# Sliding-window attention and a highway layer in one kernel: key halves by head, one pass of value products, and a new order of the work

## The chip, the core and the metric

The kernel runs on one core of a Trainium2 chip. The metric is the time of one execution on the device in microseconds (us); lower is better. The time shown is the median of several executions. A separate execution is taken with the profiler on, and all rows below come from it. The engines are TensorE (PE in the rows, with its weight loads as PEld), VectorE (DVE), ScalarE (ACT), GpSimd (POOL) and SyncE (SP). Each works through its own queue in order, and semaphores hold an instruction back until what it needs is there.

## What is computed

Eight batches of eight heads, 576 positions, 64 values a head; attention looks back over a window of 128 positions, with a slope for each head on the distance. Its output, as 4,608 tokens of 512 values, goes through a highway layer.

```python
scores = scale * np.matmul(q, k.transpose(0, 1, 3, 2))
rel = pos[:, None] - pos[None, :]
slopes = 2.0 ** (-8.0 * (np.arange(H, dtype=np.float32) + 1) / H)
mask = (rel >= 0) & (rel < window)
scores = np.where(mask, scores - slopes[:, None, None] * np.abs(rel), -1e9)
attn = np.exp(scores - max); attn = attn / (np.sum(attn) + 1e-09)
x = np.matmul(attn, v)             # then tokens x 512
H = np.maximum(x @ w_h, 0.0)
T = 1.0 / (1.0 + np.exp(-(x @ w_t + b_t)))
out = T * H + (1.0 - T) * x
```

## The kernel before

The work is cut in two ways. A **unit** (b, s) is a batch and one of four stretches of keys: two key tiles of 64 (three in the last stretch), against the 192 queries that can see each tile. There are 32 units. A **block** is 128 rows of output: (b, 0) to (b, 3) for each batch, and after each pair of batches a fifth, (b, 4), with the last 64 rows of both. There are 36 blocks. A block takes keys from its own unit and from the one before.

The order of all work is written out by hand: in `ORDER` every letter is one step, and the loop at L386 issues the steps of a letter one after the other. So the string sets the order on each engine's queue. The steps are:

- `L` load (L117), GpSimd's queue: q and k of a batch in two DMAs each, one for the even heads and one for the odd ones (batch 0 in halves of the positions, so eight), v in one. Weights are loaded once.
- `T` tr (L199), VectorE: transposes q (w = 0) or k (w = 1) of a batch in 32 x 32 blocks of words, 18 times.
- `s` scores (L216), TensorE: 32 to 48 matmuls of 32 rows x 64 columns. Which half of PSUM's partitions a key tile lands in depends on its head and its number: `half = (j + a) % 2` (L223).
- `e` soft (L238), ScalarE: exp of 1,536 scores a partition, and `m` mask (L245), VectorE: multiplies all 1,536 by `MK`, a table that holds the slopes' exponentials and the window.
- `p`, `D`, `P` (L249 to L285): the value products in two phases of 16 matmuls with a drain of TensorE between them. v lies in SBUF in its natural tiles of 128 rows, so a key tile's half is that of v. Two row halves of the array must not write one PSUM bank at a time; each phase pairs bank j with half `(j + odd) % 2`.
- `n` norm (L287), VectorE: reciprocal of the sums, which a column of ones in v gives (L291), and the product (L292).
- `x` x_tr (L298), TensorE: transposes x into a PSUM tile `f`; `c` x_copy (L304), ScalarE, to SBUF.
- `b` bias (L329), ScalarE, writes the bias into a tile `f`; `z` mm_z (L334) adds the gate product; `h` mm_h (L308) the H product, four matmuls each of 128 x 128 against 512 columns.
- `a` tanh (L346) and `r` relu (L321), ScalarE; `v` sub (L325), `y` to_gate_v (L353), `g` gate (L357), VectorE; `o` add_x (L360), GpSimd, in two halves from block 18 on; `d` store (L368), SyncE's queue.

PSUM holds one tile of scores (four banks), one of values `av` (two banks) and two tiles `f` (L98), which transposed x, gate product and H product take in turn. In SBUF q and k have three buffers, v four (`NVA`), exp'd scores eight (`NP`), x eight, and the tiles of the highway layer six each.

The mask table is made in setup3 and setup4 (L166 to L192): eight exps on ScalarE, a product on VectorE, and copies on GpSimd for the last unit's form.

Of the kernel before, what the change touches and what calls it, by code (L numbers as in the profile page):

```python
# [11 lines left out]
NLD, NTR, NVA, NP = 3, 3, 4, 8  # L12
# [4 lines left out]
GATE_S = ()  # L17

HALF_O = set()

ORDER = (
    "L1LLLLLLLLTLTLsLeTLLTLsL2e3seLsemLmpDP4mnmxpcLDP5LznLhayxrpLTDPcbzLhnaTxLrpcDPbnszeyvghv"
    "gamoxrscoydpbDPeznLdhvLgamxrsoTcpbDPeLdznhamxLrsLcvpTbDPeznhamxrsvcvpbyDPLgeyzonhaLmdxrs"
    "yycTpbDPezLhnaxLrmscvbpDPvegLznohgaxdrsmcpbDPgvoeznhoTdaxrpLdmDPcbsnzLeyghuoaxLdscmbpDPv"
    "eyzyLnLhamxrysyvcpgDPbgeznohgdamxrsgocTpbDPeLdzhLnarmxpcDPTobzodnhayxdrysyvcgpbDPvgeznoh"
    "TadxrscpbDPmezLnhyamxLrsycTopbDPeznLdhLvamLxrsgcvLpbgDPvegznohaTxrosdcpbDPmdeznohaTxdrsc"
    "mpbDPeyznhuaxscmbpDPezynhyamxrsyycvpbvDPgegznohaTodxrscpdbDPmeznhamxrsycyvpbgDPgezvnohag"
    "dxmrscpyobTDPezodnhamdxrscyvpbDPgvezgnohaxmdrscopbDPezndhyamxrysvcgpbvDPgeoznhaodxrsmcdp"
    "bDPyevznhvamxrsvcgpDPbggeznohaoudxpcDPmdbznohavdyxgrpyDPcobnzdvghayoxrpDPcgdbynozhvdagyx"
    "orpDPcbndzvghaoxrvdcybgzohadyrvgod"  # L30
# [3 lines left out]
def lists():  # L34

    units = [(b, s) for b in range(NB) for s in range(NS)]
    blocks = []
    for m in range(NB // 2):
        blocks += [(b, s) for b in (2 * m, 2 * m + 1) for s in range(NS)] + [(2 * m, NS)]
    trs = [(0, i, w) for i in range(2) for w in range(2)]  # L40
    trs += [(b, None, w) for b in range(1, NB) for w in range(2)]
    loads = [("t", 0, i, w, j) for i in range(2) for w in range(2) for j in range(2)]
    loads[8:8] = [("v", 0)]
    loads += [("w", 0), ("w", 1), ("w", 2)]
    for b in range(1, NB):
        loads += [("t", b, None, w, j) for w in range(2) for j in range(2)] + [("v", b)]
    by = dict(L=loads, T=trs)
    by.update({k: units for k in "sem"})
    by.update({k: blocks for k in "pPnxchzagod"})
    n = dict(enumerate(blocks))  # L50
    HALF_O.update(blocks[NB * 2 + 2 :])
    by["u"] = [n[i] for i in n if i not in RELU_S]
    by["r"] = by["v"] = [n[i] for i in n if i in RELU_S]
    by["b"] = [n[i] for i in n if i in BIAS_S]
    by["t"] = [n[i] for i in n if i in GATE_S]
    by["y"] = [n[i] for i in n if i not in GATE_S]
    return by
# [3 lines left out]
def kernel(  # L61
# [36 lines left out]
    ps_f = ctx.enter_context(tc.tile_pool(name="ps_f", bufs=2, space=PSUM))  # L98
# [9 lines left out]
    PB = [cp.tile([P, 64 + 256 * H], BF16, name=f"p{i}") for i in range(NP)]  # L108
# [6 lines left out]
    MK = [cp.tile([P, H, 192], BF16, name=f"mk{i}") for i in range(2)]  # L115

    def load(kind, *at):  # L117
        if kind == "t":
            b, i, w, j = at
            ld = LD[b % NLD, w]  # L120
            src = (q, k)[w][b].rearrange("(g j) n d -> j g n d", j=2)[j]
            if i is None:
                nc.gpsimd.dma_start(
                    out=ld[j::2].rearrange("p t d -> p (t d)"),
                    in_=src.rearrange("g (s t) d -> g s (t d)", t=NT))
            else:
                n = NT // 2
                nc.gpsimd.dma_start(  # L128
                    out=ld[j::2, i * n : (i + 1) * n, :].rearrange("p t d -> p (t d)"),
                    in_=src[:, i * 288 : (i + 1) * 288].rearrange(  # L130
                        "g (s t) d -> g s (t d)", t=n))
# [12 lines left out]

    def setup1():

        for i in range(NP):
            nc.vector.memset(PB[i][:, 0:64], 0.0)
            nc.vector.memset(PB[i][:, 64:].rearrange("p (h n) -> p h n", h=H)[:, :, 192:256], 0.0)
# [6 lines left out]
    rel_i = cp.tile([P, 192], I32, name="rel_i")  # L156
    dia_i = cp.tile([P, P], I32, name="dia_i")

    def setup2():

        for i in range(2):
            nc.gpsimd.iota(rel_i[i * D : (i + 1) * D, :], pattern=[[1, 192]], base=0,
                           channel_multiplier=-1)
        nc.gpsimd.iota(dia_i[:], pattern=[[1, P]], base=0, channel_multiplier=-1)

    def setup3():  # L166

        rel = cp.tile([P, 192], F32, name="rel")
        win = cp.tile([P, 192], BF16, name="win")
        ok = cp.tile([P, 192], BF16, name="ok")  # L170
        dia = cp.tile([P, P], F32, name="dia")
        nc.vector.tensor_copy(out=rel[:], in_=rel_i[:])
        for h in range(H):
            nc.scalar.activation(out=MK[0][:, h, :], in_=rel[:], func=ACTF.Exp,
                                 scale=-slopes[h])
# [8 lines left out]
        nc.vector.tensor_tensor(  # L184
            out=MK[0][:], in0=MK[0][:],
            in1=ok[:].rearrange("p (o n) -> p o n", o=1).to_broadcast([P, H, 192]), op=ALU.mult)

    def setup4():
        nc.gpsimd.tensor_copy(out=MK[1][:], in_=MK[0][:])
        for j in range(2):  # L190
            rows = slice((1 - j) * D, (2 - j) * D)
            nc.gpsimd.tensor_copy(out=MK[1][rows, j::2, 128:192], in_=MK[0][rows, 1 - j :: 2, 0:64])  # L192

    def setup5():
        pb = ps_f.tile([P, DM], F32, name="f")
# [3 lines left out]
    def tr(b, i, w):  # L199
        n = slice(0, NT) if i is None else slice(i * NT // 2, (i + 1) * NT // 2)  # L200
# [3 lines left out]
        if w:  # L204
            to = to[:, 2 * s0 : 2 * (s0 + 16 * t)].rearrange("p (s t j) -> p t s j", t=t, j=2)
# [8 lines left out]
    SC, PT, AV, X = {}, {}, {}, {}  # L214

    def scores(b, s):  # L216
        sc = SC[b, s] = ps_sc.tile([P, G, 512], F32, name="sc")
        QT = TR[b % NTR, 0][:].rearrange("p (j n) e -> p n j e", j=2)
        KT = TR[b % NTR, 1][:].rearrange("p (n j) e -> p n j e", j=2)
        for a in (2 * s, 2 * s + 1) if s < 3 else (6, 7, 8):  # L220
            for e in range(2):
                for j in range(2):
                    half = (j + a) % 2  # L223
                    n = min(192, S - a * D)
                    off = 192 * j if a < 8 else 192 * (1 - j) + 128
                    for g in range(G):
                        rows = slice(32 * g, 32 * g + 32)
                        nc.tensor.matmul(  # L228
                            out=sc[half * D : (half + 1) * D, g, off : off + n],
                            lhsT=KT[rows, a * D : (a + 1) * D, j, e],  # L230
                            rhs=QT[rows, a * D : a * D + n, j, e],
                            start=e == 0, stop=e == 1,
                            tile_position=(32 * g, half * D))

    def pview(t):
        return t[:, 64:].rearrange("p (h n) -> p h n", h=H)[:, :, 0:192]

    def soft(b, s):  # L238
        t = PT[b, s] = PB[(b * NS + s) % NP]
        nc.scalar.activation(  # L240
            out=pview(t).rearrange("p (g j) n -> p g j n", j=2),
            in_=SC.pop((b, s))[:, :, 0:384].rearrange("p g (j n) -> p g j n", j=2),
            func=ACTF.Exp, scale=scale)

    def mask(b, s):  # L245
        p = pview(PT[b, s])
        nc.vector.tensor_tensor(out=p, in0=p, in1=MK[s == 3][:], op=ALU.mult)  # L247

    def pv(b, s, odd=0):  # L249

        if not odd:
            AV[b, s] = ps_av.tile([P, 2, 512], F32, name="av")
        av = AV[b, s]
        for g in range(G):
            todo = []
            for j in range(2):
                half = (j + odd) % 2
                at = 64 + 256 * (2 * g + j)
                if s < NS:
                    own = (b, s, 2 * s + odd, at - 64 * odd, 0, P)  # L260
                    last = (b, s - 1, 2 * s - 2 + odd, at + 128 - 64 * odd, 0, P)
# [161 lines left out]
```

## Time and profile before

| | |
|---|---|
| median of 3 runs | 186.24 us (185.04 to 187.01) |
| the profiled execution, its own time | 184.66 us |
| its span, first to last instruction | 182.8 us |
| mean granted TensorE clock | 0.965 of full speed |
| GpSimd adds (L365) | 54 instructions, 50.8 us |
| DMA, software queue / hardware queue | 15.24 MB / 9.44 MB |

Spans and starts are in us from the first instruction of the profiled execution. A row of a group gives line, engine, operation, output and inputs with their shapes, the count, then busy us and the mean ns of one, then the idle time ahead of it and what ended it. A row of the timeline gives start, duration and the same names. A row of windows gives the stretch, then the busy us of PE, PEld, DVE, ACT and POOL with their counts, the granted clock and DMA. A row of waits gives who waited for whom: us in total, times, the longest. A busy share is an average over stages with different limits.

### The profile page before, as it was taken

The page shows a single profiled execution, that of the slowest core. Times are in us where ns is not written, and L with a number is a line of the kernel's source. Part 1 is how long each engine was busy: PE and PEld are TensorE (multiplying, and loading weights), DVE is VectorE, ACT ScalarE, POOL GpSimd, SP SyncE. Part 2 cuts the span into 40 slices and gives each one's busy share as a digit, 9 for nine tenths or more (in the row PEclk, how much of TensorE's full clock was granted, in tenths as well). Part 3 has the DMA queues.
Part 4 walks back from the last instruction along what each step waited for, and adds up shares of the span by engine and source line. Part 5 has one row for each costly group of instructions (what it writes and reads, how often), then busy time and mean ns, then how long its engine had stood idle before and what let it go on. Part 6 is the DMA issues. An engine that isn't in the chain of part 4 may idle for free.

```text
span 182.8 us, 6167 instructions
## 1 busy us (share of the span) xinstructions
PE 130.7 (71%) x2674; PEld 73.8 (40%) x2674; DVE 143.2 (78%) x260; ACT 123.1 (67%) x182; POOL 94.8 (52%) x111
## 2 busy tenths in 40 slices
PE   0002337897894999899399969989997899888530
PEld 0001224453462556555245544445554456444310
DVE  7027196589994899899989999989999799887520
ACT  2003852488894799889339975989997999756620
POOL 7684589108923198559210995005092742948350
PEclk9999999999997899999969987999999999999997
DMA  1899999999999999999961699990422213333122
GB/s 17 102 177 161 207 201 148 149 154 156 232 194 145 180 127 162 226 231 180 233 157 66 47 185 175 244 108 10 113 84 95 77 42 118 95 129 126 71 105 59
DMA packets 53147, 25.07 MB, mean 137 GB/s; under 512 B 45184, under 2 KB 46208, under 8 KB 53120
## 3 DMA queue, kind: packets, MB, share of 16 engines
q0 software_dynamic: 47872, 15.24, 96.4%
q1 hardware_dynamic: 5248, 9.44, 15.5%
q8 instruction: 21, 0.34, 0.8%
q14 instruction: 6, 0.05, 0.1%
HBM read 30.41 MB, written 9.44 MB: 218 GB/s over the span
## 4 chain that ended last, share of the span: by engine, by line
DVE 37%; PE 32%; ACT 13%; issue 7%; DMA 5%; POOL 3%; POOLq 0%; DVEq 0%
PE f L340 12%; DVE p L247 9%; PE f L312 9%; DVE tr L209 8%; DVE uu L358 6%; DVE x L292 5%; DMA ld<-in_k_dram 5%; PE av L278 4%; ACT f L332 4%; ACT rr L323 3%; DVE tt L354 3%; PE sc L228 3%; DVE uu L327 3%; ACT xt L306 3%; POOL ld L128 2%
## 5 line engine op out<-in xcount | busy, mean ns | idle before, releaser
L365 POOL TENSOR_TENSOR ot<-uu,x 128x256 f32<-128x256 bf16 (+1 forms) x54 | 50.8, 960 | 64.4 <-issue 33.2
L240 ACT ACTIVATE p<-sc 128x1536 bf16<-128x1536 f32 x32 | 46.7, 1458 | 16.7 <-PE sc L228 16.6
L340 PE MATMUL f<-wT,xt 128*128 128x512 bf16 x144 | 40.6, 407 | 6.0 <-ACT f L332 5.1
L312 PE MATMUL f<-wH,xt 128*128 128x512 bf16 x144 | 39.1, 396 | 0.0
L209 DVE STREAM_TRANSPOSE tr<-ld 128x1152 uint32<-128x1152 uint32 (+1 forms) x18 | 29.6, 1657 | 8.9 <-DMA ld<-in_q_dram 7.9
L228 PE MATMUL sc<-tr,tr 32*64 32x192 bf16 (+2 forms) x1152 | 21.0, 262 | 21.5 <-DVE tr L209 15.6
L278 PE MATMUL av<-va,p 64*128 64x65 bf16 (+1 forms) x1088 | 29.2, 196 | 7.1 <-issue 2.5
L247 DVE TENSOR_TENSOR p<-p,mk 128x1536 bf16<-128x1536 bf16 x32 | 33.8, 1060 | 0.3 <-ACT p L240 0.2
L348 ACT ACTIVATE tt<-f 128x512 f16<-128x512 f32 x36 | 21.7, 602 | 16.1 <-PE f L340 14.5
L306 ACT COPY xt<-f 128x512 bf16<-128x512 bf16 x36 | 21.0, 583 | 9.6 <-PE f L301 9.4
L292 DVE TENSOR_TENSOR x<-av,rd 128x512 bf16<-128x512 f32 x36 | 24.9, 692 | 3.0
L278 PEld LDWEIGHTS <-p 64*128 64x128 bf16 (+1 forms) x1088 | 20.3, 98 | 15.4 <-issue 10.3
L323 ACT ACTIVATE rr<-f 128x512 bf16<-128x512 f32 x33 | 19.7, 598 | 8.6 <-PE f L312 7.2
L228 PEld LDWEIGHTS <-tr 32*64 32x64 bf16 x1152 | 15.0, 138 | 25.2 <-DVE tr L209 16.1
L358 DVE TENSOR_TENSOR uu<-uu,tt 128x512 bf16<-128x512 bf16 x36 | 22.8, 644 | 0.7
L312 PEld LDWEIGHTS <-xt 128*128 128x128 bf16 x144 | 14.8, 103 | 19.4 <-issue 4.1
L134 POOL DMA_DIRECT2D va<-in_v_dram x8 | 15.0, 1870 | 14.6 <-PE av L278 10.5
L301 PE MATMUL f<-ident,x 128*128 128x128 bf16 x144 | 14.2, 222 | 10.1 <-DVE x L292 9.9
L332 ACT COPY f<-bB 128x512 f32<-128x512 f32 x35 | 21.2, 606 | 0.0
L340 PEld LDWEIGHTS <-xt 128*128 128x128 bf16 x144 | 13.0, 101 | 18.0 <-issue 6.2
L301 PEld LDWEIGHTS <-x 128*128 128x128 bf16 x144 | 10.5, 99 | 22.8 <-DVE x L292 14.6
L354 DVE TENSOR_SCALAR tt<-tt 128x512 f16<-128x512 f16 x36 | 14.9, 424 | 5.5 <-ACT tt L348 5.5
(38 smaller groups left out, 64.5 us busy)
## 6 DMA issues: line engine op xcount, KB each, us to landing
out_dram<-ot SPq DMA_DIRECT2D x32, 256.0 KB, 3.8
va<-in_v_dram POOLq DMA_DIRECT2D x8, 576.0 KB, 14.3
ld<-in_q_dram POOLq DMA_DIRECT2D x14, 288.0 KB, 13.9
ld<-in_k_dram POOLq DMA_DIRECT2D x14, 288.0 KB, 13.4
out_dram<-ot SPq DMA_DIRECT2D x8, 128.0 KB, 2.4
ld<-in_q_dram POOLq DMA_DIRECT2D x4, 144.0 KB, 7.1
ld<-in_k_dram POOLq DMA_DIRECT2D x4, 144.0 KB, 8.2
wH<-in_moe_w_h_dram POOLq DMA_DIRECT2D x1, 512.0 KB, 11.2
```

Source lines behind the costliest of these rows:

```text
L209: nc.vector.transpose(out=to, in_=LD[b % NLD, w][:, n].rearrange("p t d -> p (t d)").bitcast(U32).rearrange("p (t i) -> p t i", i=32))
L228: nc.tensor.matmul(out=sc[half * D : (half + 1) * D, g, off : off + n], lhsT=KT[rows, a * D : (a + 1) * D, j, e], rhs=QT[rows, a * D : a * ...
L240: nc.scalar.activation(out=pview(t).rearrange("p (g j) n -> p g j n", j=2), in_=SC.pop((b, s))[:, :, 0:384].rearrange("p g (j n) -> p g j ...
L247: nc.vector.tensor_tensor(out=p, in0=p, in1=MK[s == 3][:], op=ALU.mult)
L278: nc.tensor.matmul(out=av[o : o + n, j, g * (D + 1) : (g + 1) * (D + 1)], lhsT=PT[bb, ss][rows, col : col + n], rhs=VA[bb % NVA][rows, (9 ...
L292: nc.vector.tensor_tensor(out=x[:].rearrange("p (g j d) -> p j g d", j=2, d=D), in0=av[:, :, :, 0:D], in1=rd[:].to_broadcast([P, 2, G, D]) ...
L306: nc.scalar.copy(out=xt[:].rearrange("p c n -> p (c n)"), in_=XP.pop(at)[:, 0:512])
L312: nc.tensor.matmul(out=pa[:], lhsT=xt[:, c, :], rhs=wH[:, c, :], start=c == 0, stop=c == NC - 1)
L332: nc.scalar.copy(out=pz[:], in_=bB[:])
L340: nc.tensor.matmul(out=PZ[at][:], lhsT=xt[:, c, :], rhs=wT[:, c, :], start=c == 0 and not begun, stop=begun and c == NC - 1, skip_group_ch ...
L358: nc.vector.tensor_tensor(out=UU[at][:], in0=UU[at][:], in1=TT.pop(at)[:], op=ALU.mult)
L365: nc.gpsimd.tensor_tensor(out=ot[:, i : i + n], in0=uu[:, i : i + n], in1=x[:, i : i + n], op=ALU.add)
```

## The change

1. **Halves by head.** A key tile's half is now its head's parity `j`, for scores, exp'd scores and mask alike. q is loaded by one DMA a batch with a head's 16 partitions together; so is k of batch 0, while k of the other batches keeps two DMAs and the old layout. The transposition of q writes `p t j s` instead of `p t s j`.
2. **Odd v tiles copied.** For odd key tiles v lies in the other half. A new step `V` (copy_v) copies these tiles across partitions into `VC`, by two DMAs a batch on SyncE's queue. v gets five buffers, `VC` three.
3. **One pass of value products.** Bank j always pairs with half j, so the two phases and the drain become one step of the same matmuls.
4. **Middle slopes by TensorE.** In the middle 64 of a tile's 192 queries every position is inside the window; the slope there is added to the scores by eight small matmuls a unit (`BK`, `BQ`, 128 columns each), and the mask multiplies only the outer two thirds, 1,024 elements.
5. **x in spare value columns.** x is transposed into columns 260 to 387 of the two banks of `av` (as bf16), so `av` is given up only after x_copy. The two tiles `f` become one tile for H (`ps_h`) and one for the gate product (`ps_z`).
6. **Sums wait for VectorE.** Each GpSimd add gets a dependency on the last mask, subtraction, scaling or gate issued ahead of it; it is no longer split. A path that takes the norm's sums over ScalarE is there and unused (`SUM_S` is empty).
7. **A new order**, with the mask table made ahead of the first transpositions; more small setup steps (`BK`, `BQ`, the table by outer parts).

```diff
-NLD, NTR, NVA, NP = 3, 3, 4, 8
+NLD, NTR, NVA, NVC, NP = 3, 3, 5, 3, 8
+K_HEADS = (0,)
...
-    "L1LLLLLLLLTLTLsLeTLLTLsL2e3seLsemLmpDP4mnmxpcLDP5LznLhayxrpLTDPcbzLhnaTxLrpcDPbnszeyvghv"
+    "1LL2L3LL4LTL8LLLLTLTseT6semLV7seseLpnmxcmpmLnhLxzcrha5pbznyxaTcrpbhnzvgxocTraLvsbyyzgeVd"
...
-    "bDPyevznhvamxrsvcgpDPbggeznohaoudxpcDPmdbznohavdyxgrpyDPcobnzdvghayoxrpDPcgdbynozhvdagyx"
-    "orpDPcbndzvghaoxrvdcybgzohadyrvgod"
+    "gasyonbhegdxmozcpamdbsonrzevdxvhvcmsrgapyohnbexydzygvcmosaupbydnezgxhgcmopraohdnbxrvdzyc"
+    "ggpavohbnodxrzcydgpavhbyonzrgdvxocahbydgzroavdygod"
...
-    ps_f = ctx.enter_context(tc.tile_pool(name="ps_f", bufs=2, space=PSUM))
+    ps_h = ctx.enter_context(tc.tile_pool(name="ps_h", bufs=1, space=PSUM))
+    ps_z = ctx.enter_context(tc.tile_pool(name="ps_z", bufs=1, space=PSUM))
...
+                nc.gpsimd.dma_start(
+                    out=ld[:].rearrange("p t d -> p (t d)"),
+                    in_=src.rearrange("h (s t) d -> (h s) (t d)", t=NT))
...
             to = to.rearrange("p (j n) -> p j n", j=2)[:, :, s0 : s0 + 16 * t].rearrange(
-                "p j (s t) -> p t s j", t=t)
+                "p j (s t) -> p t j s", t=t)
...
+    def locked(op):
+        LAST[0] = op.ins.name
...
+        for j in range(2):
+            for g in range(G):
+                rows = slice(32 * g, 32 * g + 32)
+                nc.tensor.matmul(
+                    out=sc[j * D : (j + 1) * D, g, 0:384].rearrange(
+                        "p (i n) -> p i n", i=2)[:, :, D : 2 * D],
+                    lhsT=BK[rows, :],
+                    rhs=BQ[rows, j, :].rearrange("p (o n) -> p o n", o=1).to_broadcast(
+                        [32, 2, D]),
+                    start=False, stop=True, skip_group_check=True,
+                    tile_position=(32 * g, j * D))
...
     def mask(b, s):
-        p = pview(PT[b, s])
-        nc.vector.tensor_tensor(out=p, in0=p, in1=MK[s == 3][:], op=ALU.mult)
+        p = PT[b, s][:].rearrange("p g i (c n) -> p (g i) c n", n=D)[:, :, 0:3:2, :]
+        mk = MK[s == 3][:].rearrange("p g i c n -> p (g i) c n")
+        locked(nc.vector.tensor_tensor(out=p, in0=p, in1=mk, op=ALU.mult))
+
+    def copy_v(b):
+        for j in range(2):
+            m = 5 * j
+            nc.sync.dma_start(
+                out=VC[b % NVC][j * D : (j + 1) * D],
+                in_=VA[b % NVA][(1 - j) * D : (2 - j) * D].rearrange(
+                    "p (g m) d -> p g m d", m=9)[:, :, m : m + 4, :])
...
+            terms = [(b, s, 2 * s, 0, 0, P), (b, s, 2 * s + 1, 192, 0, P)]
+            if s:
+                terms += [(b, s - 1, 2 * s - 2, 128, 0, P), (b, s - 1, 2 * s - 1, 320, 0, P)]
...
+                    va = (VC[bb % NVC][rows, g, a // 2, :] if a % 2 else
+                          VA[bb % NVA][rows, (9 * (2 * g + j) + a) // 2, :])
...
+    def x_part(at):
+        return AV[at][:].rearrange("p j n -> p (j n)").bitcast(BF16).rearrange(
+            "p (j n) -> p j n", j=2)[:, :, 520:776]
...
-        nc.scalar.copy(out=xt[:].rearrange("p c n -> p (c n)"), in_=XP.pop(at)[:, 0:512])
+        nc.scalar.copy(out=xt[:].rearrange("p (j c) n -> p j (c n)", j=2), in_=x_part(at))
+        AV.pop(at)
...
-        n = DM // (2 if at in HALF_O else 1)
-        for i in range(0, DM, n):
-            nc.gpsimd.tensor_tensor(out=ot[:, i : i + n], in0=uu[:, i : i + n],
-                                    in1=x[:, i : i + n], op=ALU.add)
+        op = nc.gpsimd.tensor_tensor(out=ot[:], in0=uu[:], in1=x[:], op=ALU.add)
+        tc.add_manual_dep(op.ins, LAST[0], mybir.DependencyInfo(
+            mybir.DependencyClass.Sync, mybir.DependencyReason.DATA), reason="port")
```

In steady work the new order issues, on TensorE, for each block: value products, scores, the gate product of the block before, x's transposition, the H product of the block before. On ScalarE it is exp, copy of x, tanh, bias, relu, with shifts. Copies of v are issued one block or more ahead of their first use, but for batch 0.

More of the change, by code (lines that the diff above doesn't have):

```diff
@@ L114 @@
     ones0 = cp.tile([P, P], BF16, name="ones0")
-    MK = [cp.tile([P, H, 192], BF16, name=f"mk{i}") for i in range(2)]
+    EX = cp.tile([P, G, 192], BF16, name="ex")
+    MK = [cp.tile([P, G, 2, 2, D], BF16, name=f"mk{i}") for i in range(2)]
+    BK = cp.tile([P, D], BF16, name="bk")
+    BQ = cp.tile([P, 2, D], BF16, name="bq")
     def load(kind, *at):
@@ L336, in mm_z @@
         if not begun:
[L337 removed]
+            PZ[at] = ps_z.tile([P, DM], F32, name="z")
         xt = XT[at]
```

256 lines of the change are left out of this document (138 added, 118 removed).

## The prediction

> **What bounds the kernel now.** I read the page's busy times first, then the steady stretch as windows, then the waits and the chain that ended last.
>
> ```profile
> span 182.8 us, 6167 instructions
> ...
> PE 130.7 (71%) x2674; PEld 73.8 (40%) x2674; DVE 143.2 (78%) x260; ACT 123.1 (67%) x182; POOL 94.8 (52%) x111
> ```
> ```profile
> 37.60:171.70 134.10, 115.87 (x2413) 65.36 (x2412) 121.29 (x208) 107.39 (x157) 67.31 (x72) 0.96 1.09 140
> 40.00:130.00 90.00, 76.97 (x1598) 43.00 (x1597) 82.75 (x131) 71.56 (x103) 44.80 (x43) 0.94 1.43 162
> ```
> No engine is full over the span, but from the transposition of block 2 (37.6) to that of the last, block 35 (171.7), VectorE is busy for 121.3 of 134.1 us, TensorE for 115.9, ScalarE for 107.4. Between 40 and 130 VectorE has 82.75 of 90 us: 92%. That is the first bound.
>
> ```profile
> PE f L301 <- DVE x L292: 9.9, 9, 3.0
> ...
> PE f L340 <- ACT f L332: 5.1, 10, 1.4
> ```
> ```profile
> 165.45 0.48 ACT xt L306
> 165.92 0.50 ACT f L332
> 166.47 1.02 PE f L340 x4
> 167.49 0.88 PE f L312 x4
> 168.39 0.60 ACT rr L323
> ```
> The waits name what TensorE lacks: the norm (VectorE) 9.9 us, the bias put into PSUM 5.1. The second comes from the pool `f`: two buffers for three uses of each block. In the chain near the end, where no scores are left, copy, bias, gate product, H product and relu follow one another: 0.48 + 0.50 + 1.02 + 0.88 + 0.60 = 3.48 us a block, with hand-overs of about 0.05. So two bounds stand in turn: VectorE, then the two buffers.
>
> **The change part by part.** *Masks and sums (VectorE).*
> ```profile
> 107.10 0.95 DVE L247 TENSOR_TENSOR p<-p,mk 128x1536 bf16<-128x1536 bf16 x1
> 107.97 0.42 DVE L358 TENSOR_TENSOR uu<-uu,tt 128x512 bf16<-128x512 bf16 x1
> ...
> 108.76 1.26 DVE L358 TENSOR_TENSOR uu<-uu,tt 128x512 bf16<-128x512 bf16 x1
> ...
> 123.85 0.29 DVE L354 TENSOR_SCALAR tt<-tt 128x512 f16<-128x512 f16 x1
> ```
> ```profile
> 108.53 1.20 POOL L365 TENSOR_TENSOR ot<-uu,x 128x512 f32<-128x512 bf16 x1 [0.36 <-DVE uu L358]
> ```
> ```profile
> L240 ACT ACTIVATE p<-sc 128x1536 bf16<-128x1536 f32 x32 | 46.7, 1458 | 16.7 <-PE sc L228 16.6
> ...
> L247 DVE TENSOR_TENSOR p<-p,mk 128x1536 bf16<-128x1536 bf16 x32 | 33.8, 1060 | 0.3 <-ACT p L240 0.2
> ...
> L209 DVE STREAM_TRANSPOSE tr<-ld 128x1152 uint32<-128x1152 uint32 x14 | 25.9, 1851 | 0.0
> ...
> L358 DVE TENSOR_TENSOR uu<-uu,tt 128x512 bf16<-128x512 bf16 x36 | 22.8, 644 | 0.7
> ...
> L354 DVE TENSOR_SCALAR tt<-tt 128x512 f16<-128x512 f16 x36 | 14.9, 424 | 5.5 <-ACT tt L348 5.5
> ```
> ```profile
> L292 DVE TENSOR_TENSOR x<-av,rd x36: 691/692/693, 27.8 to 169.8; 128x512 bf16<-128x512 f32 x36
> ```
> 1,536 elements cost 0.95 us and 512 cost 0.42, so 1,024 cost about 0.68. A mask saves 0.27: 28 masks in the steady stretch, 7.6 us.
>
> The gate at 108.76 lasts 1.26 instead of 0.42 and overlaps a GpSimd add from 108.53: it is held until that add is nearly done. Summed against the clean prices: masks 33.8 − 32 × 0.95 = 3.4, gates 22.8 − 36 × 0.42 = 7.7, scalings 14.9 − 36 × 0.29 = 4.5; 15.6 us together. The change makes each add wait for the last such VectorE step ahead of it. It can still meet the next one. Reading the new order, after 26 of the 36 adds VectorE goes on with a norm, a transposition or another step that reads PSUM or one operand (norms are not stretched: 691 to 693 ns, all 36), after 9 with a mask, subtraction, scaling or gate, after the last with nothing. 9 × 0.84 = 7.6 us stay, 8 go. Bounds: 0, if collisions only move, and 15.6. Behind a waiting add on GpSimd stand the next adds and loads, and on the store queue the stores; GpSimd is 52% busy and loads run batches ahead, so I cost that at nothing; without this cover it is one VectorE step a load, up to 1.85.
>
> VectorE: 121.3 − 7.6 − 8 = 105.7.
>
> *Transpositions by DVE.*
> ```profile
> L209 DVE STREAM_TRANSPOSE tr<-ld x18: 745/1370/2337, 12.5 to 137.4; 128x1152 uint32<-128x1152 uint32 x14, 128x576 uint32<-128x576 uint32 x4
> ```
> Two forms, 1.37 and 2.34 us. K writes pairs of adjacent words, q writes every word far from the last, and the long ones are the first of each pair: q. The new layout still spreads q's words, now 144 bytes apart, so I leave 2.34; the bound is 7 × 0.97 = 6.8 us less, and as much more if spreading still costs otherwise. The Trainium skill (Advanced Engine Details and Errata, SBUF Cachelines) gives 16-byte lines with a penalty when every access is on another one: by it q stays slow and the sum is as above, while by the short row it would be 6.8 lower on an engine that is no longer the bound. No run yet shows the new stride.
>
> *TensorE.*
> ```profile
> 116.55 0.40 PE L301 MATMUL f<-ident,x 128*128 128x128 bf16 x4 [0.34 <-DVE x L292]
> 116.88 0.58 PE L228 MATMUL sc<-tr,tr 32*64 32x192 bf16 x32
> 117.40 0.92 PE L278 MATMUL av<-va,p 64*128 64x65 bf16 x32
> 118.25 1.04 PE L340 MATMUL f<-wT,xt 128*128 128x512 bf16 x4
> 119.12 1.03 PE L312 MATMUL f<-wH,xt 128*128 128x512 bf16 x4
> 119.99 0.39 PE L301 MATMUL f<-ident,x 128*128 128x128 bf16 x4
> ```
> ```profile
> 37.93 0.35 PE av L278 x16
> ```
> From start to start: transposition 0.33, scores 0.52, values 0.85, the two products 0.87 each; 3.44 a block. Without the drain the values cost between 2 × 0.35 = 0.70 and 0.85; I take 0.77, which saves 33 × 0.08 = 2.6. The middle slopes add 8 short matmuls to each unit: at 0.52 / 32 each, 0.13, or two thirds of it by their columns, or double if the split output slows them; 28 × 0.13 = 3.6. TensorE: 115.9 − 2.6 + 3.6 = 116.9. The granted clock was 0.94 between 40 and 130; if fewer gaps raise it, up to 6% of 77 us go; I take half, 2.3: 114.6. Its work hardly changes, but it is the largest now.
>
> *ScalarE* keeps exp, copy, relu, bias and tanh: 107.4. The exps of the mask table move ahead of the scores.
>
> *PSUM.* H and gate products get a buffer each, and the transposed x goes into free columns of the value tile `av`. The 3.48 loop is gone. What is late next: `av` is a single tile, free again only when ScalarE has copied x, not after the norm.
>
> *The start.*
> ```profile
> 19.23 1.86 POOL L134 DMA_DIRECT2D va<-in_v_dram  x1 [2.70 <-DMA va<-in_v_dram]
> ```
> ```profile
> 23.49 4.17 DVE L247 TENSOR_TENSOR p<-p,mk 128x1536 bf16<-128x1536 bf16 x3
> ```
> ```profile
> 24.66 0.89 PE L278 MATMUL av<-va,p 64*128 64x65 bf16 x16
> ...
> 37.55 0.39 PE L301 MATMUL f<-ident,x 128*128 128x128 bf16 x4
> ```
> ```profile
> out_dram<-ot SPq DMA_DIRECT2D x8, 128.0 KB, 2.4
> ```
> The first value product (24.66) now waits for masks whose table is made late. The new order makes the table while the loads run; then the batch's v decides. It lands at 19.2 (a load waited for it until then) and must be copied across: two transfers of 130 KB, and a 128 KB store takes 2.4 us to land. Bounds 21.6 and, behind other packets, 24; I take 22.5. From there to block 2's transposition it was 12.9 us. The three masks that stand until 27.7 ahead of the first norm no longer hold it (its product ended at 25.55): 2.0 less; the first two values each wait for a copy, 1.2 more. Block 2: 34.5. GpSimd has 11 load issues fewer, which nothing waits for.
>
> *The end.*
> ```profile
> 171.74 0.39 PE L301 MATMUL f<-ident,x 128*128 128x128 bf16 x4
> ...
> 178.52 1.11 SPq L376 DMA_DIRECT2D out_dram<-ot  x2
> ```
> From block 35's transposition to the end it is 11.1 us, 4.3 of them the last store. Without the bias wait the gate product ends some 2.8 us after that start (x 0.33, copy 0.48, products 1.74, hand-overs); tanh 0.60 (as the relu), scaling 0.29, gate 0.42 and one undivided add of 1.20 follow, then 4.3: 9.8 with hand-overs.
>
> **Sum.** TensorE paces; no engine paced better than VectorE's 92%, so 114.6 / 0.92 = 124.6. 34.5 + 124.6 + 9.8 = 168.9 of span. The profiled run took 184.66 against its span of 182.8, so 170.8; the median of the runs, 186.24, is 0.9% above the profiled one, so 172.
>
> **The rivals.**
> *The steady part does not gain.* Three engines within 10% of each other with one buffer for scores, values, H and gate each lose to one another what the edits save: 134.1 stays. 34.5 + 134.1 + 9.8 + 1.9 = 180.3, by the median 182. For it: ScalarE's 107.4 lies close behind. Against: the largest load falls from 121.3 to 114.6, and two named waits lose their causes.
>
> *Copies across come late.* If each later batch's first value product waits for the two transfers on the store queue, 7 × 2.4 = 17 us: 189. Against: the order issues them one block or more ahead.
>
> *The value tile becomes a serial loop: slower.*
> ```profile
> 115.52 0.19 DVE L291 RECIPROCAL rd<-av 128x8 f32<-128x8 f32 x1
> 115.81 0.69 DVE L292 TENSOR_TENSOR x<-av,rd 128x512 bf16<-128x512 f32 x1
> ```
> Values 0.85, norm 0.98, transposition 0.33, copy 0.48 and four hand-overs of 0.05: 2.84 a block, 93.7 for 33, if nothing stands ahead. But engines work in order: an exp of 1.46 can stand ahead of the copy (28 times, 40.9) and a transposition of 1.85 ahead of the norm (14 times, 25.9), 66.8 in all. Above 60% exposed the loop passes today's 134.1; at three quarters it is 143.8, and the time 192. Against: the new order puts scores and gate product (1.39) between values and transposition, more than norm and hand-overs (1.08), and the H product (0.87) over the copy. The Trainium skill (PSUM — Partial Sum Buffer, on bank collisions) asks that PSUM be guarded by bank and not by address; by that rule the next values cannot start under the copy though they write other columns, so this loop is real, where a guard by address would leave only the 114.6. No row of before shows it, as x lay in another tile.
>
> **How the numbers follow.** Forecast 172, chance 0.60, its own range 163 (TensorE 98% busy, start 1.5 earlier) to 179. No steady gain, 182: 0.20. Late copies, 189: 0.06. Serial loop, 192: 0.12. Something better than 163: 0.02. The range 162 to 184 leaves out the last three. A measurement can tell about 1%, so faster means under 184.4: 0.60 + 0.17 + 0.02 = 0.79; within 1%: 0.03 of the second case and 0.02 of the third, 0.05; slower: 0.04 + 0.12 = 0.16.
>
> **What would show it.** Masks near 0.68; VectorE's stretched steps fewer than half; no bias wait of the gate product; block 2's transposition near 34.5; TensorE over 90% busy in the steady stretch. I am wrong if values wait for the x copy, if the first product waits past 24 for the copied v, or if the norm still leads TensorE's waits.

## The result, and the profile after

The changed kernel takes 196.03 us (median of 4 runs, 194.98 to 197.44), the kernel before 186.5 beside it: a ratio of 1.053, 95% interval 1.044 to 1.062. It is slower; 172 was forecast. Runs of one kernel scatter by up to 6%, mostly with the granted clock; ratios rest on the undisturbed ones, where too few were left for an interval medians and lowest times are given instead, and the traces of e2, e6, e7, e8 and e10 below are of disturbed ones.

The stages, from the timelines of TensorE, in us; block 0's, block 2's and block 35's transposition of x mark their ends:

| | before | forecast | after |
|---|---|---|---|
| start to block 0 | 28.6 | | 34.5 |
| start to block 2 | 37.6 | 34.5 | 43.6 |
| block 2 to block 35 | 134.2 | 124.6 | 139.6 |
| block 35 to the end | 11.1 | 9.8 | 9.9 |
| span | 182.8 | 168.9 | 193.2 |

The end came as forecast. The start is 9.1 us over it and the steady stretch 15.0.

From the page of the changed kernel: the busy times, the clock and DMA in 40 slices, the DMA queues, the chain that ended last by engine and by line, and the landing times of two transfers (count, size, median us).

```profile
span 193.2 us, 6670 instructions
...
PE 129.2 (67%) x2930; PEld 74.5 (39%) x2930; DVE 125.6 (65%) x274; ACT 126.2 (65%) x185; POOL 75.5 (39%) x84
...
PE   0023201786499969991595969996693999989940
...
PEclk9999999999958999998599999999998599999996
DMA  2999999999999970079999946399999426323333
...
q8 instruction: 23, 0.38, 0.9%
...
PE 31%; DMA 19%; ACT 17%; DVE 15%; issue 12%; POOL 2%; POOLq 1%; SPq 0%; DVEq 0%
DMA vc<-va 13%; PE z L427 8%; PE h L398 8%; PE av L352 7%; DMA va<-in_v_dram 6%; DVE x L373 5%; ACT xt L391 4%; ACT p L314 4%; PE sc L294 4%; ACT z L419 4%; PE av L386 3%; ACT tt L435 3%; DVE uu L413 3%; ACT rr L409 2%; DVE p L322 2%
...
ld<-in_q_dram POOLq DMA_DIRECT2D x7, 576.0 KB, 18.2
vc<-va SPq DMA_DIRECT2D x16, 130.0 KB, 10.5
```

VectorE's busy time fell from 143.2 to 125.6, TensorE's hardly moved, and no engine is full. In the chain VectorE fell from first place to 15%. In its stead stand the copies across, `vc<-va`, with 13% of the span, and "issue" with 12%: TensorE waiting for nothing that the profile shows. A copy took 10.5 us to land at the median, where the prediction took 2.4 from a store of the same size. And in the middle of the span PE has slices at 1 and 3 tenths, each followed by one in which the clock was 5 tenths.

TensorE's waits, of the changed kernel and then of the kernel before (us in total, times, the longest):

```profile
PE av L352 <- DMA vc<-va: 17.6, 4, 9.2
...
PE av L352 <- issue: 6.6, 3, 3.0
PE sc L294 <- issue: 2.9, 1, 2.9
PE av L386 <- DVE x L373: 2.7, 6, 1.0
PE av L352 <- ACT xt L391: 2.1, 5, 0.9
PE z L427 <- ACT z L419: 1.5, 3, 0.7
PE sc L303 <- issue: 1.2, 1, 1.2
```
```profile
PE av L278 <- issue: 2.5, 1, 2.5
PE f L340 <- issue: 0.4, 1, 0.4
PE sc L228 <- issue: 0.2, 1, 0.2
```

The two waits that the change was to ease did ease: the norm from 9.9 to 2.7, the bias from 5.1 to 1.5. The new ones are larger: 17.6 for copies, and 6.6 + 2.9 + 1.2 = 10.7 of issue, where it was 3.1.

The timeline of TensorE shows where the copies were late (start, duration, and in brackets the idle time before):

```profile
30.11 0.21 PE L352 MATMUL av<-vc,p 64*128 64x65 bf16 x1 [9.17 <-DMA vc<-va]
32.90 0.21 PE L352 MATMUL av<-vc,p 64*128 64x65 bf16 x1 [2.58 <-DMA vc<-va]
...
93.50 0.21 PE L352 MATMUL av<-vc,p 64*128 64x65 bf16 x1 [5.60 <-DMA vc<-va]
```

and the chain in order of time has the transfers behind the first and the third (start, duration):

```profile
5.75 11.87 DMA va<-in_v_dram
...
18.46 14.40 DMA vc<-va
...
83.37 10.59 DMA vc<-va
```

v of batch 0 was there at 17.6, earlier than I had reckoned. Its copy across landed at 32.9. Both late copies ran while the DMA row of the page stood at 9, but for the second's first slice, at 7. The copies of the other batches follow that row too: beside loads they landed after 8.3 to 11.4 us, and those issued at 113 and 161 us, where the row stands at 4 and 6, after 2.5 to 3.7.

### The profile page after: what moved, and what is told of

Its sections match the earlier page's. It is cut to its first block, busy times and chain, and to the rows that moved or that the text cites. A ratio compares the mean times of both kernels' runs of the same rounds, so it can differ in the third digit from the quotient of the medians.

```text
span 193.2 us, 6670 instructions
## 1 busy us (share of the span) xinstructions
PE 129.2 (67%) x2930; PEld 74.5 (39%) x2930; DVE 125.6 (65%) x274; ACT 126.2 (65%) x185; POOL 75.5 (39%) x84
## 4 chain that ended last, share of the span: by engine, by line
PE 31%; DMA 19%; ACT 17%; DVE 15%; issue 12%; POOL 2%; POOLq 1%; SPq 0%; DVEq 0%
DMA vc<-va 13%; PE z L427 8%; PE h L398 8%; PE av L352 7%; DMA va<-in_v_dram 6%; DVE x L373 5%; ACT xt L391 4%; ACT p L314 4%; PE sc L294 4%; ACT z L419 4%; PE av L386 3%; ACT tt L435 3%; DVE uu L413 3%; ACT rr L409 2%; DVE p L322 2%
## 5 line engine op out<-in xcount | busy, mean ns | idle before, releaser
L448 POOL TENSOR_TENSOR ot<-uu,x 128x512 f32<-128x512 bf16 x36 | 41.8, 1169 | 103.2 <-issue 34.6
L398 PE MATMUL h<-wH,xt 128*128 128x512 bf16 x144 | 40.7, 409 | 1.1 <-ACT xt L391 0.7
L391 ACT COPY xt<-av 128x512 bf16<-128x512 bf16 x36 | 21.0, 584 | 30.7 <-PE av L386 30.6
L427 PE MATMUL z<-wT,xt 128*128 128x512 bf16 x144 | 38.4, 390 | 2.1 <-ACT z L419 1.5
L294 PE MATMUL sc<-tr,tr 32*64 32x192 bf16 (+2 forms) x1152 | 21.5, 270 | 22.8 <-DVE tr L265 12.8
L352 PE MATMUL av<-vc,p 64*128 64x65 bf16 (+1 forms) x512 | 22.7, 197 | 17.6 <-DMA vc<-va 17.6
L435 ACT ACTIVATE tt<-z 128x512 f16<-128x512 f32 x36 | 21.7, 602 | 4.9 <-PE z L427 4.5
L322 DVE TENSOR_TENSOR p<-p,mk 128x1024 bf16<-128x1024 bf16 x32 | 22.4, 719 | 2.8 <-ACT p L314 2.5
L419 ACT COPY z<-bB 128x512 f32<-128x512 f32 x35 | 20.8, 595 | 0.9
L409 ACT ACTIVATE rr<-h 128x512 bf16<-128x512 f32 x33 | 19.8, 600 | 1.2 <-PE h L398 1.2
L398 PEld LDWEIGHTS <-xt 128*128 128x128 bf16 x144 | 12.7, 102 | 12.9 <-issue 3.2
L386 PE MATMUL av<-ident,x 128*128 128x128 bf16 x144 | 15.1, 232 | 3.2 <-DVE x L373 2.7
L442 DVE TENSOR_TENSOR uu<-uu,tt 128x512 bf16<-128x512 bf16 x36 | 15.8, 460 | 0.2
## 6 DMA issues: line engine op xcount, KB each, us to landing
vc<-va SPq DMA_DIRECT2D x16, 130.0 KB, 10.5
```

The costliest lines, as they stand in the source:

```text
L294: nc.tensor.matmul(out=sc[j * D : (j + 1) * D, g, off : off + n], lhsT=KT[rows, a * D : (a + 1) * D, j, e], rhs=QT[rows, a * D : a * D + n ...
L352: nc.tensor.matmul(out=av[o : o + n, j, g * (D + 1) : (g + 1) * (D + 1)], lhsT=PT[bb, ss][rows, g].rearrange("p i n -> p (i n)")[:, at : a ...
L386: nc.tensor.transpose(out=x_part(at)[:, c // 2, (c % 2) * P : (c % 2 + 1) * P], in_=X[at][:, c * P : (c + 1) * P], identity=ident[:])
L391: nc.scalar.copy(out=xt[:].rearrange("p (j c) n -> p j (c n)", j=2), in_=x_part(at))
L398: nc.tensor.matmul(out=pa[:], lhsT=xt[:, c, :], rhs=wH[:, c, :], start=c == 0, stop=c == NC - 1)
L419: nc.scalar.copy(out=pz[:], in_=bB[:])
```

## The experiments

The first theory, A: the copies by DMA are the loss, since their packets get few turns beside the loads' packets; what they cost is a matter of the load on the DMA engines. Its rivals: the value tile as a serial loop, VectorE, the row layout. From the gaps of the profile came a second theory, C: the issue waits are blocks of TensorE's own instructions that come late, again behind load packets.

**e1: no copies.** The odd tiles of k are multiplied with the v rows that already lie in their half of the partitions; the output is another.

```
-                    va = (VC[bb % NVC][rows, g, a // 2, :] if a % 2 else
-                          VA[bb % NVA][rows, (9 * (2 * g + j) + a) // 2, :])
+                    va = VA[bb % NVA][rows, (9 * (2 * g + j) + a) // 2, :]
```


> The changed kernel without the copies of v: odd key tiles are multiplied with the v rows that lie in their half already, so the output is another one and the work on TensorE the same. Theory A (the copies wait behind the loads on the DMA engines and hold the value products): the first value product ends near 21.3 instead of 33.4 us, the 5.6 us wait at 88 us goes too; 196 - 12 - 5.6, so 177 to 181 us. Rival B (the value tile's loop and the engines among themselves set the steady pace): the start alone gains, 183 to 187 us.

**e2: copies by VectorE.** The same copies, but as one instruction for each half, across the partitions.

```
-            nc.sync.dma_start(
+            nc.vector.tensor_copy(
                 out=VC[b % NVC][j * D : (j + 1) * D],
```


> The copies of v made by VectorE (16 copies of 64 partitions x 1,040 values across the partition halves) instead of DMA. Theory A: as without copies plus 16 x 0.4 to 1.1 us on VectorE, which is not the bound, 178 to 184 us. Rival B: 184 to 190 us.

**e3: long packets.** Copies by DMA of whole rows of a partition (4,680 bytes) in place of four runs of 520 bytes for each partition: a quarter of the runs, 2.25 times the bytes.

```
-                    "p (g m) d -> p g m d", m=9)[:, :, m : m + 4, :])
+                out=VC[b % NVC][j * D : (j + 1) * D].rearrange("p m d -> p (m d)"),
+                in_=VA[b % NVA][(1 - j) * D : (2 - j) * D].rearrange("p m d -> p (m d)"))
```


> Copies stay on DMA but move the whole half row of v in one run of 4,680 bytes a partition: 2.25 times the bytes, 4 runs an engine and copy instead of 16. If a copy waits its turn packet by packet behind the loads, landing falls from 10.5 us (median) to 4 to 6 and the time to 182 to 188 us; if it is bytes that count, landing rises above 10.5 and the time stays at 196 or more.

Measured beside 185.42 for the kernel before: e1 181.67 (175.45 to 183.02), e2 181.67, ratio 0.978 (0.974 to 0.981), e3 203.98, ratio 1.096 (1.085 to 1.107). TensorE's timeline in e1, at the start:

```profile
20.73 0.62 PE L348 MATMUL av<-va,p 64*128 64x65 bf16 x16
22.38 0.61 PE L382 MATMUL av<-ident,x 128*128 128x128 bf16 x4 [1.03 <-DVE x L369]
```

The first value product now runs through, and block 0's transposition starts at 22.38 instead of 34.47: 12.1 us come from the copies of the first batches alone. e2 gets the same start (22.38), with the computation kept; its copies, by the rows of that tile (shortest, median, longest ns):

```profile
L328 DVE COPY vc<-va x16: 426/428/1286, 17.5 to 155.2; 64x1040 bf16<-64x1040 bf16 x16
```

So the change loses by its DMA copies; with VectorE's in their place it is some 2% faster than the kernel before. In e3 the copies landed after 9.0 us (median) instead of 10.5, though with 2.25 times the bytes, and TensorE again waited 17.6 us for them. Neither landing that was expected came, 4 to 6 us if the number of runs decides or above 10.5 if the bytes do, so theory A's few turns are not shown; bytes, or the backlog ahead of them, count as well. Its issue waits rose too, one of them to 7.2 us.

But even without copies e1's steady stretch was 131.4 us, against 124.6 forecast. Its issue waits add up to 11.1 us, of which 9.4 are real: the traces of e1 to e4 lack 33 of the 2,930 matmul records, and each hole looks like a wait of 0.16 to 0.34 us. The copies explain the start and some of the stretch, not the rest.

**e4: e2 with early loads.** The last fourteen loads (from the second k half of batch 4 on) stand two to seven blocks earlier in the order; nothing else moves.

```
-    "vzmcpasbnzeyTxhabysgrgzvocpagLdVhbmLenzuxasmLcvbpvoeznLdxahmLcyLvprsnbhegyxTozcpLdasbLyn"
+    "mbxyrvzmcpLasbnzeyTxhabysgrgzvocpagdVhbmenzuxasmcvbpLLvoezndxahmcyvpLLrsnbhegyxTozcpdasb"
```

> Copies by VectorE, and the last fourteen loads issued four to eight blocks earlier, so that the DMA engines are idle in the second half. Theory C (gaps of 1.2 to 3.0 us in the middle of TensorE's matmul runs are late fetches of instruction blocks behind the loads): the gaps after 100 us, 9.5 us of the 10.7, mostly go; 5 to 9 us less than with the late loads. Rival: the gaps have nothing to do with the loads, and the two are within 1.5 us.

179.49, ratio 0.965 (0.957 to 0.973). Behind 100 us one issue wait of 0.79 was left; but ahead of it the waits grew to 3.26, 2.96, 1.38, 1.19 and 1.51, and the sum stayed: 12.8, or 11.3 without the holes. By the undisturbed runs e4 is 1.8 us faster than e2, not the 5 to 9 expected: the stalls moved with the loads to where these were put. It is also the best complete version of the study, level with e7.

**e5: e4 without the late loads.** The q and k loads of batches 3 to 7 and the v loads of batches 5 to 7 are left out, all else stays; the output is another.

```
             b, i, w, j = at
+            if b >= 3:
+                return
...
             b, = at
+            if b >= 5:
+                return
```


> e4 without the q and k loads of batches 3 to 7 and the v loads of batches 5 to 7: the buffers keep what they held, so the output is another. All instructions of TensorE, VectorE and ScalarE stay. Theory C (TensorE stands still, under the name issue, because blocks of its instructions are fetched late behind load packets): the issue waits on TensorE fall from 11 to 13 us (e4: 12.8) to under 2 us, the instruction fetches stay 23 in number, and the time falls to 168 to 172 us. Rival (the stalls come with the instruction stream itself, whatever the DMA engines do): issue waits stay above 5 us and the time at 176 us or more, apart from 1 to 2 us of memory contention.

**e11: the changed kernel without the late loads.** The same cut in the changed kernel, copies by DMA kept.

> The changed kernel as it is, copies by DMA, without the q and k loads of batches 3 to 7 and the v loads of batches 5 to 7 (the buffers keep what they held, so the output is another). The loads of the start stay. Theories A and C together: the first value product still waits some 12 us for the copies of batches 0 and 1 (first x at 33 to 35 us), the second wait of 5.6 us near 88 us goes, the issue waits fall to under 2 us, and the time is 178 to 184 us, about the 12 us of the start above e5. Rival (copies are slow by themselves, whatever the loads): waits for the copies of 4 us or more stay after 60 us, and the time is above 186 us.

**e9: the kernel before without the late loads.** The same cut, as a control.

> The kernel before without the q and k loads of batches 3 to 7 and the v loads of batches 5 to 7 (the buffers keep what they held, so the output is another); the control of e5. If the late loads cost the changed kernel more than the kernel before (theory C: the kernel before had only 3.1 us of issue waits, because its TensorE often waited for VectorE while its instructions arrived): the time falls by 2 to 5 us, to 180 to 184 us, and VectorE stays the bound. Rival (loads slow any kernel alike): it falls by 9 to 11 us, as e5 did against e4, to 174 to 177 us.

e5: 169.33 (168.73 to 170.37), ratio 0.917 (0.906 to 0.928). e11: 175.55 (175.09 to 175.66), ratio 0.953 (0.949 to 0.957). e9: 178.53 (178.38 to 178.89), ratio 0.970 (0.966 to 0.974). The issue waits are 1.9 us in e5 and none in e11 and e9. The steady stretch of the changed kernel and of e11 as windows (stretch, length, busy us of PE, PEld, DVE, ACT and POOL with counts, then clock, DMA and GB/s):

```profile
43.60:183.30 139.70, 114.19 (x2638) 65.63 (x2637) 105.05 (x209) 108.50 (x158) 56.36 (x53) 0.93 1.27 142
```
```profile
44.30:163.90 119.60, 109.57 (x2637) 63.28 (x2636) 105.03 (x209) 107.87 (x158) 41.77 (x35) 0.97 0.61 102
```

The same matmuls, within one, take 139.7 with the loads and 119.6 without them. The 20 us are the issue waits, 10.7; the copy waits near 90 us, 5.9; and TensorE's own slower matmuls at the lower clock, 114.19 − 109.57 = 4.6: 21.2, of which about one was idle time anyway. VectorE and ScalarE were not slowed. TensorE is busy for 91.6% of e11's stretch: the pace that the prediction put into its sum is there once the late loads are gone. The copies are fast there too: the four beside the loads of the start landed after 10.7 to 14.9 us, the other twelve after 2.5 to 5.3.

For the kernel before the same cut is worth 182.8 − 176.6 = 6.2 us of span, against 193.2 − 173.9 = 19.3: the loads cost both, but the changed kernel three times as much. My 180 to 184 for e9 was too high: issue waits were only half of what the loads cost there. VectorE's clashes fell too (gates from 22.8 to 21.4 us, scalings from 14.9 to 12.4), with 23 load issues fewer on GpSimd. In e11 the start kept its loss, as expected (block 0 at 35.2, with 12.8 us of waiting for copies), but my range was a little high.

**e10: loads in pieces.** e2 with the loads of batches 3 to 7 cut up and two pieces issued behind each block, the same bytes.

```
+        elif kind == "q":
+            b, r = at
+            rows = slice(r * D, (r + 1) * D)
...
+            m = slice(0, 36) if len(at) == 1 else slice(9 * at[1], 9 * at[1] + 9)
```


> e2 (copies by VectorE) with the loads of batches 3 to 7 cut up: q in two row halves, v in four parts of nine rows of 128 keys, and two pieces issued behind each block's value product from block 2 to block 22. The same bytes, spread evenly. Theory C in the form that a fetch waits for the backlog of load packets: with a short backlog the issue waits fall to 4 to 8 us (e4: 12.8) and the time to 172 to 177 us. Rival (a fetch waits its turn among the packets whatever the backlog, as long as some load is in flight): issue waits 10 us or more, time 178 to 183 us.

181.59, ratio 0.975 (0.963 to 0.987); its lowest run, 178.73, is no lower than e4's 178.53, and the issue waits are 12.2. The forecast fell, but the run does not tell its two theories apart: the pieces, too, took 11.8 to 12.7 us to land (medians), and the DMA row stands at 9 in nearly every slice up to 122 us, so the backlog never was short. Its timeline shows what the waits are. TensorE, from one to the next (the value products from 57.85 on are 16 rows of two, of which the first and the last are shown):

```profile
53.70 0.21 PE L374 MATMUL av<-va,p 64*128 64x65 bf16 x1 [4.49 <-issue]
53.70 0.26 PE L374 MATMUL av<-vc,p 64*128 64x65 bf16 x2
53.90 1.89 PE L449 MATMUL z<-wT,xt 128*128 128x512 bf16 x4
55.58 0.63 PE L408 MATMUL av<-ident,x 128*128 128x128 bf16 x4
56.00 1.91 PE L420 MATMUL h<-wH,xt 128*128 128x512 bf16 x4
57.85 0.24 PE L374 MATMUL av<-va,p 64*128 64x65 bf16 x2
...
58.46 0.19 PE L374 MATMUL av<-vc,p 64*128 64x65 bf16 x2
58.59 0.58 PE L316 MATMUL sc<-tr,tr 32*64 32x192 bf16 x32
58.99 0.24 PE L325 MATMUL sc<-bq,bk 32*64 32x128 bf16 x8
59.16 1.04 PE L420 MATMUL h<-wH,xt 128*128 128x512 bf16 x4
60.03 0.39 PE L408 MATMUL av<-ident,x 128*128 128x128 bf16 x4
60.81 0.58 PE L316 MATMUL sc<-tr,tr 32*64 32x192 bf16 x32 [0.39 <-ACT p L336]
61.16 0.21 PE L325 MATMUL sc<-bq,bk 32*64 32x128 bf16 x1
62.36 0.26 PE L325 MATMUL sc<-bq,bk 32*64 32x128 bf16 x7 [0.97 <-issue]
```

From the first stall to the second stand 1 + 2 + 4 + 4 + 4 + 32 + 32 + 8 + 4 + 4 + 32 + 1 = 128 matmuls, 256 instructions with the weight load of each. Both stalls cut a run of like matmuls in two at a point where the kernel has no wait. The changed kernel's 2,930 matmuls and 2,930 weight loads are 22.9 times 256, and its page has 23 instruction packets; the kernel before, with 2 × 2,674, makes 20.9 and has 21. The 0.38 MB of the row, over 23, are 16.5 KB each. So the stalls stand at the borders of instruction blocks.

The traces also keep every DMA packet by itself, and the instruction packets show how a stall comes about. Counted from 0, the five stalls of the changed kernel stand before matmuls 735, 1,375, 1,503, 2,015 and 2,271, each 95 past a multiple of 128, and so do all seven of e10. Each ends 1.3 to 2.0 us after an instruction packet has landed: in the changed kernel the 5th, 10th, 11th, 15th and 17th, which are the multiples of 128 in those numbers. In e11, once the last load has landed (90.9 us), a packet starts between 0.5 us before and 1.6 us after TensorE begins the block ahead of the one that it brings, and has landed 1.29 us or more before that one is due. In the changed kernel the five packets behind the stalls start 3.7 to 5.6 us after that point. The transfer itself is no longer, 1.06 us at the median against 1.17. So a fetch begins about one block ahead, and beside loads its start is late. A late start costs nothing where TensorE is slow over the block: the changed kernel's second packet started 4.0 us after, but TensorE took 12.5 us, and no stall followed.

What holds the start back was not shown; a turn among load packets on a shared DMA engine is the likely way. The Trainium skill (DMA: Bandwidth & Descriptors, Queues, rings and completion order) has each DMA engine go round its queues packet by packet; no run here shows that this turn is what a fetch waits for. It (Runtime: NRT & Kernel Launch, Instruction fetch mechanics) also gives blocks of 16 KiB, 256 instructions, as seen here, and calls the price of crossing a border mostly hidden: in e11 it is, at no issue wait at all; under the loads it was not, with single stalls of up to 4.5 us in e10 and 7.2 in e3.

Three runs take the other parts one by one.

**e8: the kernel before, its adds waiting.** Only the new dependency: each GpSimd add waits for the last VectorE mask, subtraction, scaling or gate.

```
+            tc.add_manual_dep(op.ins, LAST[0], mybir.DependencyInfo(
+                mybir.DependencyClass.Sync, mybir.DependencyReason.DATA), reason="port")
```


> The kernel before, with one edit: each GpSimd add waits for the last VectorE operation ahead of it in program order. My forecast priced the end of collisions at 8 us of VectorE's time. If these collisions bound the kernel before, gate and subtraction fall to some 460 and 340 ns and the time to 177 to 182 us. Rival (the kernel before is not bound by them, or the add's lateness costs as much): 184 to 188 us.

**e6: e4 without that dependency.**

> e4 without the dependency of each GpSimd add on the last VectorE operation, so that the add may run beside VectorE operations again, as in the kernel before. If collisions are real but VectorE is no longer the bound: VectorE's busy time rises by 5 to 10 us (gate and subtraction near the 640 and 420 ns of the kernel before), GpSimd's adds lengthen, and the time stays within 1 percent of e4 (178 to 181 us). Rival (VectorE bounds, as in the kernel before): 183 to 188 us.

**e7: e4 with the full mask.** The mask over three parts of 64 columns as before, and no middle-slope matmuls.

```
-        p = PT[b, s][:].rearrange("p g i (c n) -> p (g i) c n", n=D)[:, :, 0:3:2, :]
+        p = PT[b, s][:].rearrange("p g i (c n) -> p (g i) c n", n=D)[:, :, 0:3, :]
```


> e4 with the mask over all three 64-column parts, as before, and without the middle-slope matmuls: VectorE takes on about 32 x 0.27 = 8.6 us, TensorE loses 264 matmuls (about 3.6 us by their 13.7 ns step) and some 528 instructions, two fetch blocks of 23. If TensorE's stream and its fetches set the pace: time 176 to 180 us, no slower than e4. Rival (VectorE is the bound, and the slopes on TensorE were what freed it): 183 to 188 us.

e8: 179.92 (176.69 to 183.47) beside 187.33 (183.62 to 189.74) for the kernel before; no interval, but by the medians 4.0% and by the lowest runs 3.8% faster, for one edit. Its VectorE groups (busy us, mean ns):

```profile
L363 DVE TENSOR_TENSOR uu<-uu,tt 128x512 bf16<-128x512 bf16 x36 | 16.1, 460 | 0.7
...
L359 DVE TENSOR_SCALAR tt<-tt 128x512 f16<-128x512 f16 x36 | 12.5, 361 | 4.3 <-ACT tt L353 4.3
```

The gates lose 22.8 − 16.1 = 6.7 us and the scalings 2.4; the subtractions gain 1.7 (14.1 to 15.8). That is the easing forecast, nearly as large as the 7 us of time. e6 stays open: 184.52 by the median, 3% over e4, but its runs lie between 179.18 and 188.77, and the lowest is 0.4% above e4's. VectorE's busy time rose as expected, from 134.9 to 140.8 us, but not in the gates (466 ns in e4, 444 in e6): the masks went from 719 to 842 ns and the copies from 484 to 604. In that trace, then, it is not the wait that keeps the gates of the new order short. e7: 179.51, ratio 0.969 (0.949 to 0.989), no different from e4. Its chain and its mask, for which VectorE takes 30.2 us instead of 22.4:

```profile
DVE 49%; PE 24%; ACT 11%; issue 10%; DMA 3%; POOLq 1%; DVEq 0%
...
L312 DVE TENSOR_TENSOR p<-p,mk 128x1536 bf16<-128x1536 bf16 x32 | 30.2, 963 | 1.1 <-ACT p L304 0.9
```

VectorE took on what TensorE was spared, and the time did not move: the middle slopes are a trade without gain here.

## Why the prediction was wrong

**The copies, the step that failed first.** "Bounds 21.6 and, behind other packets, 24; I take 22.5": the landing was priced by a 128 KB store that took 2.4 us. v came at 17.6 instead of 19.2, but the copies landed 10.5 us (median) and up to 14.4 after their issue, and the first value product, which should have had its copied tiles at 22.5, got them at 30.1 and 32.9. That was the prediction's own sign of being wrong: a first product that waits past 24 for the copied v. The mechanism, waiting for v and its copy, was named; its size was off four- to sixfold. The 2.4 was the median of eight stores, six of them from times when the DMA row stood at 0 to 3; the two beside loads, issued at 82.7, took 7.3 and 8.3 us. The copy ran among loads, and in the kernel before those of 144 KB at the start had taken 7.1 and 8.2 us (medians): these were the nearer rows. Without the copies block 0 came at 22.4 (e1, e2). The cost: 12.1 us at the start and 5.9 later, though the rival with late copies had looked for them at later batches only.

**The pace, the second.** "TensorE paces; no engine paced better than VectorE's 92%, so 114.6 / 0.92 = 124.6" took the 92% as the limit of engines that wait for one another. The busy times came out: TensorE 114.2 against 114.6, VectorE 105.05 against 105.7, ScalarE 108.5 against 107.4. For TensorE that was partly luck: 114.6 stood for a raised clock, and half of 6% was taken off for it, but over the steady stretch the clock fell from 0.96 to 0.93; at 0.97 the same work takes 109.6 (e11). What the sum lacked is a term for TensorE waiting on its own instructions, 10.7 us. TensorE was busy for 82% of the stretch, not for over 90. With the late loads out the stretch takes 119.6 us, 5 under the forecast (e11). The kernel before showed the stall too, 2.5 us once at 57 us, but its TensorE often waited for VectorE, and a fetch behind such a wait costs nothing; that reading fits e8, where an easier VectorE came with 6.0 us of issue waits, and the changed kernel's second packet, and was not tested further.

**What held.** The masks took 0.72 us for 0.68. Of the stretching of VectorE's steps the gates kept 36 × 0.04 = 1.4 us, the scalings 1.8 and the masks 1.2: 4.4 of the 7.6 that I left; the subtractions, which the sum left out, rose from 14.1 to 15.3. q's transpositions did not change (14 of both forms: 25.3 us after, 25.9 before). The bias wait fell to 1.5; the end was 9.9 for 9.8.

**The queues, put at nothing.** GpSimd's and SyncE's queues were left uncharged for waiting adds. That did not hold for batch 3. Its v had landed at 69.3, its buffer was free at 70, and the DMA row stands at 0 from 72 to 82 us, but in the order its copies follow block 4's store on SyncE's queue, and that store waited for its add. The add ran at 80.76, the store was issued at 82.18, the copies at 82.68; loads behind the same add on GpSimd's queue began at 82.10, and the copies ran beside them for 10.6 us. The new dependency made only some 0.8 us of this, as block 4's gate ended near 80.0; the rest is the order. Issued ten microseconds earlier, these copies would have met idle DMA engines; that was not run.

**The rivals.** The value tile as a serial loop costs 2.1 us, where that rival added 143.8 − 134.1 = 9.7: the copy of x was seldom late. The Trainium skill's rule (PSUM — Partial Sum Buffer, on bank collisions), to guard by bank and not by address, is one that the kernel keeps: it gives up the value tile only after that copy, and the order hides the wait. What the chip would do without that guard no run here shows. "The steady part does not gain" gave 134.1 for that stretch and the chip 139.6, but not for its reason: the engines do not lose to each other what the edits save, as e11's 119.6 shows.

**The sum, part by part,** from the runs: the waiting adds are worth some 7 us (e8); the new start, with its layout and order, about 6 (block 0 at 22.4 instead of 28.6); the middle slopes nothing (e7). Against it stand 18 us for copies by DMA and, against the kernel before, 10.7 − 3.1 = 7.6 us more of late instructions. The parts were measured in different kernels and overlap, so they don't add up to the 10.4 us of span by the last digit.

## What to carry to other kernels

Price a transfer by rows of the stretch in which it will run, with the same neighbours on the DMA engines, never by one from a quiet stretch; if a small on-chip move stands at the head of a chain, an engine that can do it in half a microsecond is worth its time. Look past a median, too: the slow stores were in the group. Before counting on a higher pace of TensorE, look for "issue" waits that cut a run of like matmuls: every 256 instructions a block must come in, its fetch begins only about one block ahead, and beside loads it begins late. An add on GpSimd that meets VectorE's two-operand steps can cost both more than letting it wait.

## What the runs showed of the hardware

A copy of 130 KB inside SBUF on SyncE's queue took 2.5 to 14.4 us to land in the changed kernel, the longer times beside loads; e3's 292.5 KB took 3.5 to 15.4. VectorE moved 64 x 1,040 bf16 values from one half of the partitions to the other in 0.43 us (median of 16, e2). TensorE's instructions came in packets of 16 KB, one for 128 matmuls and their weight loads. With no load in flight a packet started within 1.6 us of TensorE's entry into the block before, and the border cost nothing (e11); beside loads it could start 3.7 to 5.6 us after, and five of the changed kernel's borders cost 1.2 to 3.0 us each, one of e3's 7.2. In the middle of the changed kernel's span the granted clock fell to 5 tenths in three slices of 4.8 us, each next to one in which TensorE was busy for 4, 1 or 3 tenths; behind the gap of 2.87 us at 136.7 no drop is seen.
